# Token order in a linear-attention kernel: eight-token rows for k and r, values of two batches in chunk order, 64-row transposes

## The chip, the cores and the metric

The kernel runs on one core of one Trainium2 chip. The metric is device time in microseconds of one execution, the median of the runs. Five engines work side by side, each with its own instruction queue: PE (matrix products and transposes, into PSUM), DVE and ACT (vector work, both may read PSUM), POOL (vector work in SBUF) and SP (issues the DMAs). Within a queue the order is fixed; between queues semaphores order the work.

## The reference

A recurrent attention with a decaying state, then a token-mixing layer. Shapes: r, k, v, w are 4 batches x 8 heads x 768 tokens x 48, float32; the output is 4 x 768 x 384.

```python
state = zeros(B, H, D, D)
for t in range(S):
    cur = einsum('bhd,bhe->bhde', u[None] * k[:, :, t], v[:, :, t])
    y[:, :, t] = einsum('bhd,bhde->bhe', r[:, :, t], state + cur)
    state = w[:, :, t, :, None] * state + einsum('bhd,bhe->bhde', k[:, :, t], v[:, :, t])
x = y.transpose(0, 2, 1, 3).reshape(B, S, H * D)
wq = x @ w_q;  wk = x @ w_k
W_tok = (1 / sqrt(64)) * einsum('bsd,btd->bst', wq, wk)
out = maximum(einsum('bst,btd->bsd', W_tok, x), 0) @ w_out
```

## The kernel before

**Units.** A batch is cut into three units of 256 tokens; there are 12 units, n = 0 to 11. A unit holds two chunks of 128 tokens. In a chunk the recurrence is done as matrix products: with cumulative sums of log w, the weights exp(c) and exp(-c) are put on r and k, a masked 128 x 128 product per head gives the part inside the chunk, and a 48 x 48 state per head carries the rest. After the third unit of a batch the mixing layer of that batch is done.

**Loads** (L291 to L302). One DMA of 384 KB each brings w, k, r and v of a unit into the tiles wg, kg, rg, vg. A partition gets two neighbouring tokens of all eight heads, so a contiguous piece in memory is 2 x 48 x 4 = 384 bytes. For the batch in WHOLE (L233, batch 3) v comes at once, in chunk order, into vw: four DMAs, each into 64 partitions, in pieces of 192 bytes.

**Steps of a unit**, by the names of the step list, with the engine:

- ln (ACT, L453): log of w into lw. k16, r16 (L463) and v16 (L556): casts to bfloat16, on POOL mostly, of unit 0 on DVE.
- cw (PE): cumulative sums, 16 matmuls with 64 rows. ep, en (ACT, L491, L496): exp of them and of their negatives, to bfloat16. ep is written one token further on, since r needs the weight of the token before.
- kT, rT (PE, L502): k16 and r16 transposed, eight 128 x 128 transposes each. ks (ACT or DVE): copy of kT out of PSUM.
- qT (DVE, L522): r times k. RT (DVE, L531): r times ep. KT (POOL or DVE, L539): ks times en.
- vp (PE, L564): a product with the permutation PM that puts the two-token rows of v into chunk order, then VB (ACT): its copy out of PSUM. For batch 3 VB is cast from vw by POOL (L550) and there is no vp.
- dps (PE), dd: the part of a token's own key; Vd (POOL, L588): that part times VB.
- A (PE, L604), AM (DVE, L608): the products of a chunk, masked by US. kb (PE, L617), kd (L623): KT transposed back, scaled.
- sn (PE), SB (DVE, L654): the state. yi, ya (PE): both parts of the output of the recurrence. X (DVE, L712): their sum with Vd.
- xt (PE, L724), XT: X transposed. qk (PE), QK: products with w_q and w_k.
- For a batch: T, TS; then for each of its units mx (PE, L794), rl (relu, into MX), fp (PE, L812: times w_out), os (copy out), st (SP, L824: store of 384 KB).

In unit 11 and in part in unit 0 the steps are done by chunk, so that the pipeline starts and ends sooner; the suffix of a name such as AM.0.0 is the unit and the chunk. The matmuls with 64 or 48 rows use a part of the rows of PE's array, and two of them can be in the two halves.

**Order.** Each step is added to a plan with the engines it may run on. ALT (a string) picks the engine where there is a choice, RANK (a list with one number for each step) gives the place in its engine's queue. So the order of each queue is written out beforehand; a step whose input is late holds up what stands behind it. The durations in the plan (`dur`) are used to choose PSUM banks and the order in which the instructions are put into the program.

**Buffers.** PSUM is eight banks; a step takes one ("s") or two ("w"). The load tiles are rings of four, most others rings of two, so SP's loads wait for the last reader of the unit four before.

**Start.** Nine products with Z keep PE busy until the first data are there; twelve more of them (z) are spread over the order. POOL and DVE build the masks CM, US, PM and the identity.

Of the kernel before, what the change touches and what calls it, by code (L numbers as in the profile page):

```python
# [33 lines left out]
class Plan:  # L34
# [12 lines left out]
    def add(self, key, engs, fn, after=(), buf=None, reads=(), lag=None, mode=0, behind=None):  # L47
        e = next(iter(engs)) if len(engs) == 1 else next(self.alt, "")
        e = e if e in engs else next(iter(engs))
        if lag is None:  # L50
            lag = 260 if e == "E" else 80
        s = dict(key=key, engs=engs, eng=e, dur=engs[e], fn=fn, lag=lag, mode=mode, rank=0,
# [113 lines left out]
    0, 0, 0, 0, 0, 20, 0, 0, 21, 1, 3, 1, 0, 0, 2, 0, 0, 3, 0, 0, 6, 0, 0, 1, 1, 2, 3, 3, 2, 4, 6,  # L166
    6, 9, 3, 6, 4, 2, 5, 7, 5, 20, 10, 24, 12, 8, 10, 15, 8, 19, 11, 16, 9, 17, 11, 25, 12, 28,
    14, 30, 32, 35, 31, 18, 57, 30, 75, 38, 4, 0, 0, 5, 0, 0, 8, 0, 0, 7, 0, 0, 5, 4, 7, 14, 7, 8,
    18, 27, 9, 15, 16, 10, 6, 23, 14, 34, 17, 12, 38, 20, 41, 22, 26, 13, 33, 17, 36, 19, 42, 45,
    43, 46, 24, 64, 33, 77, 39, 9, 0, 0, 10, 0, 0, 13, 0, 0, 15, 0, 0, 13, 9, 20, 29, 15, 16, 37,  # L170
    44, 19, 25, 23, 13, 14, 47, 24, 51, 27, 20, 49, 26, 54, 29, 48, 25, 52, 27, 58, 68, 61, 65,
    35, 74, 37, 78, 40, 81, 43, 86, 44, 91, 47, 47, 0, 0, 88, 45, 97, 50, 51, 0, 0, 111, 56, 120,
    60, 54, 0, 0, 12, 0, 0, 11, 0, 0, 17, 0, 0, 16, 0, 0, 18, 11, 16, 40, 23, 22, 39, 56, 21, 31,
    30, 15, 17, 55, 29, 63, 34, 22, 60, 32, 67, 36, 53, 28, 66, 34, 71, 38, 70, 72, 73, 80, 41,
    89, 46, 101, 55, 14, 0, 0, 18, 0, 0, 21, 0, 0, 24, 0, 0, 21, 18, 35, 50, 28, 26, 59, 76, 31,
    40, 39, 33, 24, 84, 43, 82, 42, 28, 98, 53, 83, 44, 69, 36, 90, 47, 95, 52, 103, 104, 106,
    105, 57, 119, 63, 136, 68, 22, 0, 0, 19, 0, 0, 23, 0, 0, 27, 0, 0, 37, 19, 23, 79, 42, 41, 62,
    85, 32, 45, 46, 26, 27, 94, 49, 96, 51, 30, 102, 56, 93, 50, 92, 49, 100, 54, 108, 113, 115,
    112, 61, 129, 66, 139, 71, 145, 75, 153, 77, 160, 81, 50, 0, 0, 162, 82, 189, 97, 53, 0, 0,
    173, 88, 190, 98, 52, 0, 0, 26, 0, 0, 25, 0, 0, 30, 0, 0, 32, 0, 0, 48, 25, 31, 99, 53, 52,  # L180
    87, 110, 48, 60, 59, 32, 33, 116, 58, 122, 63, 40, 117, 62, 121, 64, 114, 57, 124, 65, 128,
    68, 132, 135, 133, 134, 72, 141, 74, 172, 87, 28, 0, 0, 29, 0, 0, 36, 0, 0, 33, 0, 0, 51, 29,
    37, 107, 54, 55, 109, 126, 58, 67, 69, 36, 35, 123, 62, 138, 69, 42, 137, 73, 144, 76, 125,
    66, 131, 71, 147, 77, 149, 150, 152, 151, 79, 164, 85, 180, 91, 35, 0, 0, 31, 0, 0, 37, 0, 0,
    34, 0, 0, 61, 34, 38, 127, 65, 64, 118, 130, 59, 70, 75, 41, 39, 143, 73, 140, 70, 47, 157,
    82, 146, 78, 142, 72, 155, 81, 166, 168, 169, 170, 88, 177, 92, 192, 101, 203, 103, 212, 105,
    218, 113, 55, 0, 0, 214, 106, 227, 111, 56, 0, 0, 222, 109, 230, 113, 57, 0, 0, 39, 0, 0, 41,
    0, 0, 38, 0, 0, 45, 0, 0, 46, 0, 0, 67, 43, 44, 148, 78, 76, 154, 158, 80, 84, 85, 48, 51,
    167, 84, 52, 176, 91, 165, 87, 163, 83, 175, 90, 179, 92, 182, 185, 184, 183, 95, 200, 102,
    211, 109, 42, 0, 0, 43, 0, 0, 40, 0, 0, 74, 46, 45, 156, 80, 79, 159, 161, 83, 86, 89, 49, 53,  # L190
    171, 86, 55, 191, 100, 181, 94, 178, 93, 187, 96, 194, 101, 197, 202, 198, 199, 104, 210, 104,
    215, 110, 48, 0, 0, 44, 0, 0, 49, 0, 0, 90, 50, 54, 186, 93, 94, 95, 96, 174, 188, 89, 99, 97,
    56, 98, 58, 57, 193, 100, 59, 60, 196, 102, 206, 105, 195, 99, 201, 103, 205, 208, 204, 207,
    209, 213, 106, 216, 108, 219, 221, 108, 112, 107, 217, 107, 220, 223, 111, 110, 224, 226, 225,
    114, 228, 115, 117, 231, 233, 114, 118, 58, 0, 0, 61, 0, 0, 229, 112, 116, 234, 235, 116, 117,
    59, 0, 0, 60, 0, 0, 232, 115, 118, 236, 237, 119, 119, 120, 62, 0, 0, 1, 2, 4, 5, 7, 8, 10,
    11, 12, 13, 21, 22,
]
ALT = "DDDPDAAAAAAPPDDAADAAPAAPAAADADAAAAAAPPDPAADADPAADADADAPPAPADDAAAAAAAAAPPDPAAADAPPDPAADAAPPAPAAAAAAADAAAAPPDPAAADPPDPADADPPAPPAADADADADDDAAADAAADDA"
# [5 lines left out]
def kernel(  # L205
# [27 lines left out]
    WHOLE = (3,)  # L233
# [18 lines left out]
    EW = 132  # L252
# [26 lines left out]
    ID16 = const([C, C], BF16, "ID16")  # L279
    IDU = const([C, C], BF16, "IDU")  # L280
# [4 lines left out]
    pos0 = const([C, 1], I32, "pos0")  # L285
    pos1 = const([C, 1], I32, "pos1")
# [8 lines left out]

    def load_whole(b, q, tl):
        n_ = H // 2 * NCH
        for j in range(2):
            nc.sync.dma_start(
                out=view(tl, q * n_ * D, [[D, n_], [1, D]], p0=64 * j, pn=64),  # L300
                in_=dataclasses.replace(v, offset=(b * H * S + j) * D + q * n_ * C * D,
                                        ap=[[D2, 64], [C * D, n_], [1, D]]))  # L302

    def setup():
# [9 lines left out]
        for j in range(2):  # L314
            nc.gpsimd.iota(pos0[ds(64 * j, 64), :], pattern=[[0, 1]], base=j,
                           channel_multiplier=2)
            nc.gpsimd.iota(pos1[ds(64 * j, 64), :], pattern=[[0, 1]], base=j + 1,
                           channel_multiplier=2)
# [3 lines left out]
        for c in range(2):  # L322
            for j in range(2):
                m = view(CM, j * C, [[64, 2], [1, 64]], p0=c * 64, pn=64)
                nc.gpsimd.affine_select(m, m, pattern=[[1, 2], [2, 64]], compare_op=ALU.is_ge,
                                        fill=0.0, base=-j, channel_multiplier=-2)
        nc.vector.memset(ID16, 0.0)
        nc.gpsimd.affine_select(ID16, ID16, pattern=[[1, C]], compare_op=ALU.not_equal, fill=1.0,
                                base=0, channel_multiplier=-1)
        for x in (tiles["lw"][0], tiles["k16"][0], tiles["r16"][0]):  # L330
            nc.vector.memset(view(x, D, pads), 0.0)
        for x in tiles["ep"]:
            nc.vector.memset(view(x, 0, [[EW, 8], [1, 1]]), 1.0)
        nc.vector.memset(US, 1.0)
        for j in range(2):
            m = view(US, 0, [[64, 2], [1, 64]], p0=j * 64, pn=64)
            nc.gpsimd.affine_select(m, m, pattern=[[1, 2], [2, 64]], compare_op=ALU.is_gt,
                                    fill=0.0, base=-j, channel_multiplier=-2)
# [4 lines left out]
        nc.vector.tensor_scalar_mul(US, US, gv)  # L343
# [5 lines left out]
    def permute():  # L349
        for c in range(2):  # L350
            for j in range(2):
                m = PM[ds(c * 64, 64), ds(j * C + j * 64, 64)]
                nc.gpsimd.affine_select(m, m, pattern=[[1, 64]], compare_op=ALU.not_equal,
                                        fill=1.0, base=0, channel_multiplier=-1)
# [14 lines left out]
    def bank():  # L369
        return Buf("s")  # L370
# [511 lines left out]
```

## Time and profile before

| | us |
|---|---|
| median of 3 runs | 106.43 (106.07 to 106.51) |
| span of the profiled execution | 104.4 |
| PE busy | 93.2 (89%) |
| PE weight loads | 69.4 (66%) |
| DVE busy | 84.4 (81%) |
| ACT busy | 80.6 (77%) |
| POOL busy | 69.3 (66%) |

The span is from the first to the last instruction of one profiled execution; the runs are timed from outside and are some 2 us longer. Busy time is the time in which an engine has an instruction running, whatever it waits for inside; matmuls overlap, so PE's figure says little of how near its peak it is. The page also cuts the span into 40 slices of 2.6 us. One row there is the TensorE clock that was granted, in tenths: it is 9 in all slices but one, at about 27 us, where it is 5. The DMA row is at 9 until the 24th slice with few exceptions and falls to 0 at about 81 us. The DMA queue that SP feeds moved 24.19 MB in 56,224 packets, 84.3% of the span of 16 DMA engines.

### The profile page before, as it was taken

The numbers are of one execution on the slowest core, as the hardware profiler recorded it, in microseconds if no ns is written. First come the engines' busy times: TensorE is split into PE (matmuls) and PEld (weight loads), VectorE is DVE, ScalarE is ACT, GpSimd is POOL, SyncE is SP. The second block draws the span as 40 slices with busy tenths as digits, with TensorE's granted clock in tenths as the row PEclk, the third lists the DMA queues.
The fourth block names the chain that finished last, engine by engine and source line by source line (L and its number), as shares of the span: only waits on it lengthen the run. The fifth ranks groups of instructions, "written<-read, shape, count | busy, mean of one in ns | idle before, by whom it ended". The sixth has DMA issues, their size and how long they took to land.

```text
span 104.4 us, 3964 instructions
## 1 busy us (share of the span) xinstructions
PE 93.2 (89%) x1651; PEld 69.4 (66%) x1652; DVE 84.4 (81%) x140; ACT 80.6 (77%) x122; POOL 69.3 (66%) x80
## 2 busy tenths in 40 slices
PE   5999899766998999999999899999999998999910
PEld 2356488544777786767886776887888596866500
DVE  6669996995789979979999889999899699695320
ACT  6348988759879869999999886899897954855830
POOL 6607666979998828959995699999975973000000
PEclk9999999999589999999999999999999999999999
DMA  1999999999999988999999799999993056004791
GB/s 26 296 324 325 325 318 234 309 290 237 301 342 295 246 228 206 303 254 243 310 294 256 195 264 276 244 179 172 292 349 137 0 220 238 0 9 181 295 359 72
DMA packets 56803, 24.65 MB, mean 236 GB/s; under 512 B 54480, under 2 KB 55632, under 8 KB 56784
## 3 DMA queue, kind: packets, MB, share of 16 engines
q1 hardware_dynamic: 56224, 24.19, 84.3%
q8 instruction: 13, 0.21, 0.8%
q10 hardware_dynamic: 560, 0.20, 0.7%
q14 instruction: 6, 0.05, 0.1%
HBM read 19.66 MB, written 4.72 MB: 234 GB/s over the span
## 4 chain that ended last, share of the span: by engine, by line
PE 74%; DMA 6%; POOL 5%; DVE 5%; issue 3%; ACT 2%; SPq 1%; POOLq 0%; DVEq 0%
PE PS L240 74%; DMA vg<-in_v_dram 6%; DVE KT L539 2%; POOL KT L539 2%; POOL v L556 2%; POOL Vd L588 1%; ACT ep L491 1%; ACT MX L396 1%; DVE RT L531 1%; DVE AM L608 1%; SPq L292 1%; DVE qT L522 1%; ACT os L384 0%; DVE Z L306 0%; POOL r L463 0%
## 5 line engine op out<-in xcount | busy, mean ns | idle before, releaser
L608 DVE TENSOR_TENSOR AM<-PS,US 128x1024 bf16<-128x1024 f32 x24 | 29.3, 1219 | 3.4 <-PE PS L240 3.2
L539 POOL TENSOR_TENSOR KT<-ks,en 128x1024 bf16<-128x1024 bf16 (+1 forms) x11 | 20.5, 1864 | 3.6 <-DVE ks L390 3.4
L588 POOL TENSOR_TENSOR Vd<-VB,dd 128x768 bf16<-128x768 bf16 (+1 forms) x14 | 18.1, 1294 | 1.3 <-ACT dd L384 1.2
L712 DVE SCALAR_TENSOR_TENSOR X<-PS,gx,Vd 128x768 bf16<-128x768 f32 (+1 forms) x13 | 12.4, 952 | 2.8 <-POOL Vd L588 1.4
L240 PEld LDWEIGHTS <-KT 48*128 48x128 bf16 (+1 forms) x272 | 10.9, 97 | 5.2 <-issue 2.4
L496 ACT ACTIVATE en<-PS 128x1024 bf16<-128x1024 f32 (+1 forms) x14 | 12.6, 898 | 2.0 <-PE PS L240 2.0
L491 ACT ACTIVATE ep<-PS 128x1024 bf16<-128x1024 f32 (+1 forms) x14 | 12.7, 919 | 1.3 <-ACT XT L384 0.6
L453 ACT ACTIVATE lw<-wg 128x768 bf16<-128x768 f32 x12 | 10.2, 848 | 4.5 <-DMA wg<-in_w_dram 4.4
L240 PE MATMUL PS<-wo,MX 128*128 128x384 bf16 x72 | 13.3, 326 | 0.0
L463 POOL CAST k<-kg 128x768 bf16<-128x768 f32 x11 | 9.0, 825 | 3.3 <-DMA kg<-in_k_dram 3.3
L384 ACT COPY os<-PS 128x768 f32<-128x768 f32 (+1 forms) x13 | 8.6, 680 | 2.5 <-PE PS L240 2.2
L463 POOL CAST r<-rg 128x768 bf16<-128x768 f32 x9 | 7.5, 835 | 4.3 <-DMA rg<-in_r_dram 2.3
L556 POOL CAST v<-vg 128x768 bf16<-128x768 f32 x9 | 7.4, 825 | 3.6 <-DMA vg<-in_v_dram 3.6
L240 PE MATMUL PS<-RT,KT 48*128 48x128 bf16 x192 | 9.7, 221 | 0.0
L240 PEld LDWEIGHTS <-MX 128*128 128x128 bf16 x72 | 6.5, 98 | 4.1 <-issue 0.3
L531 DVE TENSOR_TENSOR RT<-PS,ep 128x1024 bf16<-128x1024 bf16 (+1 forms) x14 | 8.4, 607 | 0.8 <-PE PS L240 0.5
L396 ACT ACTIVATE MX<-PS 128x768 bf16<-128x768 f32 (+1 forms) x11 | 8.2, 755 | 0.7 <-PE PS L240 0.6
L522 DVE TENSOR_TENSOR qT<-PS,ks 128x1024 bf16<-128x1024 bf16 x12 | 8.2, 681 | 0.4 <-issue 0.4
L240 PE MATMUL PS<-Z 128*128 128x512 bf16 x20 | 7.4, 511 | 1.2 <-DVE uT L309 1.2
L384 ACT COPY XT<-PS 128x768 bf16<-128x768 bf16 (+1 forms) x9 | 6.9, 765 | 2.0 <-PE PS L240 2.0
L240 PE MATMUL PS<-ID,r 128*128 128x128 bf16 x96 | 7.7, 226 | 0.4 <-POOL r L463 0.3
L240 PE MATMUL PS<-VB,AM 128*128 128x48 bf16 x192 | 7.9, 184 | 0.1
(83 smaller groups left out, 201.1 us busy)
## 6 DMA issues: line engine op xcount, KB each, us to landing
wg<-in_w_dram SPq DMA_DIRECT2D x12, 384.0 KB, 5.4
kg<-in_k_dram SPq DMA_DIRECT2D x12, 384.0 KB, 5.9
rg<-in_r_dram SPq DMA_DIRECT2D x12, 384.0 KB, 5.9
vg<-in_v_dram SPq DMA_DIRECT2D x9, 384.0 KB, 5.8
out_dram<-os SPq DMA_DIRECT2D x9, 384.0 KB, 3.0
vw<-in_v_dram SPq DMA_DIRECT2D x4, 288.0 KB, 6.2
out_dram<-os SPq DMA_DIRECT2D x5, 192.0 KB, 2.7
wof<-in_moe_w_out_dram SPq DMA_DIRECT2D x1, 576.0 KB, 5.4
```

What stands on the lines that cost most here:

```text
L240: return nc.tensor.matmul(o, l, rr, start=start, stop=stop, skip_group_check=True, is_transpose=trans)
L384: nc.scalar.copy(o, i)
L453: nc.scalar.activation(view(lw.tile, 0, [[64, H], [512, 2], [1, D]]), view(g["wg"].tile, 0, [[D2, H], [D, 2], [1, D]]), ACT.Ln, bias=0.0, ...
L463: op(view(o.tile, 0, [[64, H], [512, 2], [1, D]]), view(g[src].tile, 0, [[D2, H], [D, 2], [1, D]]))
L491: nc.scalar.activation(view(ep.tile, cs[0] * NP * EW + 66, [[EW, NP * len(cs)], [-65, 2], [1, 64]]), at(cw)[:, ds(cs[0] * 512, w_)], ACT.E ...
L496: nc.scalar.activation(en.tile[:, ds(cs[0] * 512, w_)], at(cw)[:, ds(cs[0] * 512, w_)], ACT.Exp, bias=0.0, scale=-1.0)
L531: nc.vector.tensor_tensor(view(RT.tile, cs[0] * 512, [[C, n4], [64, 2], [1, 64]]), view(at(rT, BF16), cs[0] * 512, [[C, n4], [64, 2], [1, ...
L539: x.tensor_tensor(KT.tile[:, cols], ks.tile[:, cols], en.tile[:, cols], ALU.mult)
L556: v16s = add(("v16", n), {"P": 826}, lambda e: nc.gpsimd.tensor_copy(view(v16.tile, 0, [[D, H], [DM, 2], [1, D]]), view(g["vg"].tile, 0, [ ...
L588: nc.gpsimd.tensor_tensor(Vd.tile[:, cols], VB.tile[:, cols], view(dd.tile, cs[0] * H, [[1, len(cs) * H], [0, D]]), ALU.mult)
L608: AMs[c] = add(("AM", n, c), {"D": 1221}, lambda e, c=c, A=A: nc.vector.tensor_tensor(view(AM[c].tile, 0, [[C, 8], [1, C]]), view(at(A), 0 ...
L712: nc.vector.scalar_tensor_tensor(view(X.tile, (2 * i + c0) * DM, [[DM, nc_], [1, DM]]), view(at(y), 0, [[512, nc_], [1, DM]]), gx, view(Vd ...
```

## The change

- k and r are loaded with eight neighbouring tokens of one head to a row (`load_runs`), two heads to a partition: contiguous pieces of 1536 bytes. w, and v where it isn't loaded whole, stay as they were.
- Within a chunk the tokens are therefore in another order: column 16 j + p is token 8 p + j. The masks CM, US and PM, the token numbers behind gx and gv and the moving operand of mx are made to match; the stores write rows of 1536 bytes in place of 3072.
- kT and rT become 16 transposes each, of 64 rows by 128, with a 64-column permuting identity IDP, into one pair of banks, kr, for both.
- ep is written in one piece, 16 columns further on; a new copy sh on POOL brings its last row of 15 columns to the front of each block. RT waits for sh.
- KT of units 0 and 11 is taken by DVE from PSUM directly, without ks (DIRECT).
- kb and xt get a second form ("e"): transposes in halves of 64 rows (48 for kb) into two banks. ALT chooses; kb takes it 9 times of 13, xt 6 of 13.
- WHOLE is batches 2 and 3: v of both is loaded in chunk order, by eight DMAs a batch, each into 16 partitions.
- The casts k16 and r16 of unit 0 go from DVE to POOL. RANK and ALT are new: one more k16 and two more r16 on POOL, KT 9 times on POOL instead of 11. In SP's queue the stores st.2.0, st.0.0 and st.3.0 stand ahead of the load of rg for unit 11, where it was st.0.0 alone.
- The setup has two iotas instead of four, some small integer steps on DVE for the token numbers, and IDP's masks instead of US's.

```diff
-    WHOLE = (3,)
+    DIRECT = (0, N - 1)
+    WHOLE = (2, 3)
...
-    EW = 132
+    EW = 144
...
+    def load_runs(b, i, tl, ap):
+        nc.sync.dma_start(
+            out=view(tl, 0, [[8 * D, 2], [1, 8 * D]]),
+            in_=dataclasses.replace(ap, offset=(b * H * S + i * U) * D,
+                                    ap=[[8 * D, U // 8], [2 * S * D, NP], [S * D, 2],
+                                        [1, 8 * D]]))
+
     def load_whole(b, q, tl):
...
+        nc.sync.dma_start(
+            out=view(tl, 0, [[D, H * NCH], [1, D]], p0=16 * q, pn=16),
+            in_=dataclasses.replace(v, offset=(b * H * S + q) * D,
+                                    ap=[[8 * D, 16], [C * D, H * NCH], [1, D]]))
...
+        nc.vector.tensor_scalar(US, tok, pos0, gv, ALU.is_gt, ALU.mult)
...
-                op(view(o.tile, 0, [[64, H], [512, 2], [1, D]]),
-                   view(g[src].tile, 0, [[D2, H], [D, 2], [1, D]]))
+                op(view(o.tile, 0, [[128, 8], [64, 2], [1, D]]),
+                   view(g[src].tile, 0, [[D, 8], [8 * D, 2], [1, D]]))
...
+            def f_sh(e, cs=cs, n4=n4):
+                nc.gpsimd.tensor_copy(view(ep.tile, cs[0] * NP * EW + 1, [[EW, n4], [1, 15]]),
+                                      view(ep.tile, cs[0] * NP * EW + C, [[EW, n4], [1, 15]]))
...
+        kr = wide()
+
+        def transposed(name, src, step, place):
             def f(e):
...
+                o = at(kr, BF16)
+                for j in range(8):
+                    for c in range(2):
+                        mm(view(o, c * 1024 + place + j * 16, [[C, NP], [1, 16]]),
+                           src.tile[ds(c * 64, 64), ds(j * 128, 128)],
+                           IDP[ds(c * 64, 64), :], trans=True)
...
+                if n in DIRECT:
+                    nc.vector.tensor_tensor(o, turned(0, cs[0], len(cs)), y, ALU.mult)
...
             x = add(("RT", n, cs[0]), {"D": 150 + int(n4 * C * 0.524)}, f_RT,
-                    [rTs] + [eps[c] for c in cs], RT, [rT, ep])
...
+                    [rTs] + [shs[c] for c in cs], RT, [kr, ep])
...
+                    for hh in range(2):
+                        mm(at(kb, BF16)[:, ds(hh * 1024 + cp * D, D)],
+                           KT.tile[ds(hh * 64, D), ds(cp * C, C)],
+                           ID16[ds(hh * 64, D), ds(hh * 64, D)], trans=True)
...
+                        for hf in range(2):
+                            rows = ds(hf * 64, 64)
+                            mm(at(xt, BF16)[:, ds(hf * 1024 + (dt * nc_ + k_) * 64, 64)],
+                               X.tile[rows, x], ID16[rows, rows], trans=True)
...
-                       view(QK.tile, ii * QS, [[64, 2], [C, 2], [1, 64]]),
+                       view(QK.tile, ii * QS, [[C, 2], [1, 16], [16, 8]]),
```

## The prediction

> **What bounds the kernel now.** I read the windows first, then the waits, then single instructions. Columns of the windows: stretch, its length, busy us (instructions) of PE, PEld, DVE, ACT, POOL, then granted clock, DMA share, GB/s.
>
> ```profile
> 10.68:30.00 19.32, 16.55 (x308) 12.38 (x308) 16.08 (x24) 15.69 (x23) 15.81 (x16) 0.91 1.08 292
> 30.00:60.00 30.00, 28.91 (x577) 22.74 (x574) 27.16 (x41) 27.24 (x36) 23.68 (x23) 1.00 0.99 260
> 60.00:80.00 20.00, 19.39 (x429) 16.16 (x424) 18.76 (x26) 17.21 (x28) 17.98 (x15) 1.00 1.00 248
> 80.00:90.11 10.11, 9.81 (x192) 7.62 (x190) 8.38 (x13) 6.91 (x13) 6.40 (x7) 1.00 0.32 122
> 90.11:104.40 14.29, 9.58 (x84) 6.13 (x81) 6.44 (x13) 7.38 (x15) 0.00 (x0) 1.00 0.45 167
> ```
>
> Three things are full at once: the DMA share is 0.99 to 1.08 until 80 us, PE is 96% busy from 30 us, DVE 91% from 30 to 60 and 94% to 80. No single engine owns the time. I therefore time the step that all meet, X.11.1 (DVE L712, start 90.11 us): every earlier DVE instruction stands ahead of it, and behind it lie 14.3 us of the last mixing. Between AM.0.0 (10.68) and X.11.1 DVE is busy 16.08 + 27.16 + 18.76 + 8.38 = 70.4 of 79.4 us and idle 9.0.
>
> ```profile
> DVE AM L608 <- PE PS L240: 3.2, 7, 1.1
> DVE X L712 <- POOL Vd L588: 1.4, 2, 0.9
> DVE X L712 <- PE PS L240: 1.3, 3, 0.7
> ```
> ```profile
> POOL v L556 <- DMA vg<-in_v_dram: 3.6, 4, 2.2
> POOL k L463 <- DMA kg<-in_k_dram: 3.3, 3, 1.8
> POOL r L463 <- DMA rg<-in_r_dram: 2.3, 2, 1.9
> ```
>
> DVE's idle time (first fence, waits of DVE: total us, times, longest) ends mostly on PE; POOL's (second) on loads. The longest wait for rg is the very last load: POOL sits until 79.52, where the cast of rg.11 starts. So a slow load delays POOL, POOL delays PE, PE delays DVE.
>
> **Loads.** Rates by packet size, as windows of the trace of before:
>
> ```profile
> 10.00:20.00 10.00, 8.95 (x179) 6.59 (x179) 8.77 (x14) 8.43 (x13) 7.27 (x9) 1.00 1.09 296
> 67.20:71.00 3.80, 3.63 (x74) 3.23 (x71) 3.64 (x6) 3.53 (x5) 3.80 (x4) 1.00 1.08 184
> 101.20:102.40 1.20, 0.00 (x0) 0.00 (x0) 0.00 (x0) 0.00 (x0) 0.00 (x0) 1.00 0.89 327
> ```
>
> The first moves 384-byte packets (two tokens), the second 192-byte packets of the chunk-order values, the third 1536-byte rows of the last stores. Divided by the DMA share: 272, 170 and 367 GB/s. A load of 393,216 bytes takes 1.45 us in two-token rows; in eight-token rows (8 x 48 x 4 = 1536 bytes) 1.07 us, if loads do as well as those stores: 24 loads x 0.38 = 9.1 us less. Bounds: nothing (272 GB/s again) to 9.1. Values of a batch in chunk order, 1.18 MB, take 6.9 us at 170 GB/s against 3 x 1.45 = 4.35 for three vg loads: 2.6 more for the batch that changes. In SP's queue two more stores now stand ahead of rg.11 (st.2.0 and st.3.0): 2 x 1.07 = 2.1 more. Net -9.1 + 2.6 + 2.1 = -4.4: rg.11 is cast from about 75.1 us instead of 79.5. SP issues 16 vw DMAs instead of 4, at about 0.5 us (the first kg issue at 1.28 took 0.57): 6 us more on SP, behind which wg.9 to wg.11 wait; hidden, since SP's loads at present take 1.1 to 1.2 us each because the queue is full.
>
> **PE.** Columns of the timeline: start, us, instruction; the step from one start to the next is what PE spends.
>
> ```profile
> 15.17 0.62 PE L240 MATMUL PS<-CM,lw 64*128 64x128 bf16 x16
> 15.63 0.26 PE L240 MATMUL PS<-SB,RT 48*128 48x48 bf16 x4
> 41.49 0.61 PE L240 MATMUL PS<-ID,k 128*128 128x128 bf16 x8
> 41.94 0.49 PE L240 MATMUL PS<-QK,TS 128*128 128x256 bf16 x3
> 82.91 0.40 PE L240 MATMUL PS<-RT,KT 48*128 48x128 bf16 x8
> 83.23 0.35 PE L240 MATMUL PS<-wk,XT 128*128 128x64 bf16 x6
> 84.55 0.40 PE L240 MATMUL PS<-RT,KT 48*128 48x128 bf16 x8
> 84.78 0.26 PE L240 MATMUL PS<-SB,RT 48*128 48x48 bf16 x8
> 84.98 0.57 PE L240 MATMUL PS<-VB,AM 128*128 128x48 bf16 x16
> ```
>
> Eight full transposes take 0.45 us (56 ns each). Sixteen 64-row matmuls of 128 columns take 0.46 (29 ns: two at a time). Eight RT,KT take 0.23 before another 48-row group and 0.32 before a full one: a change of row mode costs 0.09. So eight SB,RT of 48 columns take 0.20 - 0.09 = 0.11, 14 ns each. A 64-row transpose of 64 columns lies between 14 and 29; on the line through (48, 14) and (128, 29) it takes 17. kT and rT: 24 groups x (0.45 - 16 x 0.017) = -4.3 (bounds -5.4, and +0.2 at 29 ns). The order gives 9 of 13 kb steps the halved form (five with 4 columns blocks, four with 8): 52 blocks' worth of 56 ns become pairs of 14 to 17 ns, -1.3; 6 of 13 xt steps (six transposes, 0.33 to about 0.19): -0.8. The permuting matmuls vp of three units go (0.43 at 40.28, with a mode change): -1.1. Mode changes rise from 92 to 96: +0.4. Together about -7 us of PE's 93. mx (L795) reads its moving operand with a stride of 16 elements; no row shows one. From no cost (0.33 a step at 41.94) to double (the half rate that the first matmuls on Z show, 0.43 us apart against 0.22 later): 0 to +0.33 on each of 12, three of them in the tail. I take 0, since the clock alone explains the slow row.
>
> [...]
>
> **POOL.** It gains k16.0, r16.0 and one more r16 (+2.5 at 0.83 each), loses two KT net (20.5 us to 9 x 2.13 = 19.2: -1.3), v16 becomes VB at the same 0.83, and the new copy sh comes 14 times: 120 elements a row lie between the casts of 8 (0.19) and 192 elements (0.34), so 0.28, 0.23 for the four halves: +3.7. Sum +4.9 on 69.3. Each sh is queued behind casts that wait for loads, and RT (DVE), then A (PE), wait for it: this cover is what loads 4.4 us earlier pay for.
>
> **DVE and ACT.** Start: k16.0 and r16.0 leave DVE; kg.0 lands 0.4 us earlier, but DVE then does KT.0.0, ks.0, KT.0.1, kd.0.0, RT.0.0, qT.0 (four of 0.42, two of 0.68, each start some 0.05 before the last end) from the end of en.0.0 at 7.17: 2.8 to 2.9 us, AM.0.0 at about 10.1 instead of 10.68: **-0.6**. From there to X.11.1: ks.3, ks.6 and ks.9 go and ks.5 comes (-1.36), KT -0.25, RT.0.1 +0.42, one XT more +0.55, dd +0.33, TS and QK -1.1: **-1.4**. ACT takes two ks (+2.0), QK and TS (+2.4), and gives three VB, kd, two dd, r16 and XT (-6): lighter by 1.6.
>
> **Idle time of DVE** (9.0 us): PE has 7 us less to do, the loads come 4.4 us earlier, POOL is 4.9 fuller. Bounds: 0 and 5.9 (all three waits shown above). I take **-1.6**, nearer to nothing, as DVE would then be 90% busy, what it reaches now only in the middle. **Tail** of 14.3: two halved xt and earlier mx.8, **-0.4** (bounds -0.8 and +1.0, three strided mx).
>
> Sum: -0.6 - 1.4 - 1.6 - 0.4 = -4.0. The profiled execution has a span of 104.4, the median of the runs is 106.43, 2.0 more around it. Forecast: span 100.4, time **102.4**. Its own range, all bounds together: -8.7 to -1.0, 97.7 to 105.4.
>
> **Rivals.**
> *Sixteen-partition loads are slow (slower).* Each vw DMA now writes 16 partitions instead of 64. In the second window above, 64 partitions and half the packet cost 38% of the rate (170 against 272). Its forty slices, in GB/s:
>
> ```profile
> GB/s 251 235 226 174 150 119 105 95 95 125 117 117 152 202 379 226 226 212 226 232 224 218 186 138 113 115 133 137 178 156 158 210 212 228 232 212 220 208 230 192
> ```
>
> At the lowest, 95, a batch takes 12.4 us, 5.5 more than reckoned; for two batches the last load comes 2 x 5.5 - 4.4 = 6.6 us later than now, 86.1. The last vw.9 stands two transfers ahead, about 84.0, and from VB.9 on POOL still has 3 VB, k16, r16, two Vd, two sh and the halves of Vd.11: 5 x 0.83 + 2 x 1.48 + 0.46 + 1.62 = 9.2, to 93.2 instead of 87.1. X.11.1 follows at 93.3, 3.2 later than now, less 0.4 in the tail: 109.2. At 120 GB/s a batch takes 9.8 us, POOL ends at 88 and nothing is lost at this place. So it decides once the last load lands after about 83. For it: POOL can do nothing else first, as its queue is in order. Against it: half the slices show 200 to 232 GB/s on half the partitions. Time 109.2.
>
> [...]
>
> *POOL takes the gain (about even).* From k16.0 at 5.75 it has the 65.9 us that it does after 8.42 now, and 4.9 more: 76.6 without a wait. With the 12.8 us that it idles there now it ends at 89.4, 2.3 later than at present, and X.11.1 follows at 89.5: -0.6, less 0.4 in the tail, 105.4; any further 0.5 of waiting for sh's sources makes it no change. For it: in-order casts with sh behind them. Against: 9.2 of its idle time ended on loads.
>
> *The halved transposes do not pair (small gain).* PE saves 2 to 3 us, DVE's idle time stays: -0.6 - 1.4 = -2.0, the tail as now, 104.4. For it: no row has 64-row transposes. Against: CM,lw and SB,RT both pair.
>
> **Chances.** Forecast 0.52, no pairing 0.10, POOL 0.14, slow loads 0.24. Within 0.5% (0.53 us, what a measurement here can tell) lies half of POOL's. Faster: 0.52 + 0.10 + 0.07 = 0.69; same 0.07; slower 0.24. The range for 8 in 10 leaves out the far end of the slow loads and the forecast's best: 99.4 to 108.0.
>
> **What would show it.** Right: kg and rg about 1.1 us apart on the queue, the last cast of rg near 75 us; kT groups of 16 in about 0.27 us; sh near 0.28; AM.0.0 near 10; X.11.1 near 86.5. Wrong: vw at some 100 GB/s, VB waiting for vw for 5 us or more; RT waiting for sh; the granted clock at half for longer than the 3 us around 27 us in which PE, idle 1.59 us before, fell to it now.

## The result and the profile after

The changed kernel takes **121.75 us** (120.09 to 124.02, 4 runs) against 106.47 (106.07 to 106.99) of the kernel before on the same chip: ratio 1.143, 95% interval [1.132, 1.154]. Forecast were 102.4, with a range of 99.4 to 108.0: the direction was wrong, and the time lies outside the range. Ratios here and below leave disturbed runs out, which medians keep.

The span of the profiled execution is 120.1 us (before 104.4). The marker of the prediction, X.11.1, starts at 99.22 instead of 90.11. So 9.1 us were lost ahead of it and 6.6 behind it. Four lines of the page of the changed kernel: the granted clock and the GB/s of its forty slices, and two of the costliest groups (count, busy us, mean ns of one, idle time before and its releaser).

```profile
PEclk9998599999999955999999999997559999678699
GB/s 61 339 333 337 347 345 329 316 347 349 314 213 299 221 197 78 123 107 280 299 352 370 199 184 173 176 198 267 0 5 64 67 5 170 98 0 134 125 207 191
L250 PE MATMUL PS<-QK,TS 128*128 128x256 bf16 x36 | 18.3, 634 | 0.1
L419 ACT ACTIVATE MX<-PS 128x768 bf16<-128x768 f32 (+1 forms) x11 | 7.8, 723 | 12.6 <-PE PS L250 12.6
```

The third line was not among the costliest groups before. It is mx. Its 36 matmuls, three to each of the twelve steps, are now reported with 634 ns each, and ACT, which takes their results, waits 12.6 us for them. PE's timeline of the changed kernel around the first two steps (start, us, instruction):

```profile
40.27 0.37 PE L250 MATMUL PS<-VB,AM 128*128 128x48 bf16 x8
40.48 1.54 PE L250 MATMUL PS<-QK,TS 128*128 128x256 bf16 x3
41.84 0.50 PE L250 MATMUL PS<-VB,AM 128*128 128x48 bf16 x8
42.17 1.03 PE L250 MATMUL PS<-ID,KT 128*128 128x128 bf16 x8
43.13 0.61 PE L250 MATMUL PS<-RT,KT 48*128 48x128 bf16 x8
43.67 0.38 PE L250 MATMUL PS<-UB,qT 128*128 128x2 bf16 x8
43.91 1.54 PE L250 MATMUL PS<-QK,TS 128*128 128x256 bf16 x3
```

From the start of mx to the next instruction it is 1.36 us (40.48 to 41.84), where it was 0.33. From one of its matmuls to the next the trace has 440 and 460 ns; before it was 109. Twelve steps x 1.03 = 12.4 us. The waits of the changed kernel (us in total, times, longest) show who pays:

```profile
ACT MX L419 <- PE PS L250: 12.6, 10, 2.8
DVE SB L714 <- PE PS L250: 6.8, 6, 2.8
...
POOL k L489 <- DMA kg<-in_k_dram: 2.2, 2, 1.7
...
POOL VB L598 <- DMA out_dram<-os: 2.1, 1, 2.1
```

DVE's largest wait was AM's, 3.2 us; now SB waits 6.8 us: sn, which it follows, stands in PE's queue behind mx and the fp that comes after it (mx at 43.91, fp at 45.27, sn at 47.32, SB at 47.89 after 2.76 us of waiting). POOL's waits for loads have shrunk as forecast (kg 3.3 to 2.2, vg 3.6 to 0.3, none for rg), but a new one is there: VB waits 2.1 us. The releaser named is a store that was long done by then; the last packets of vw start at 80.63 us, and this cast (VB.9) at 81.40, so it is vw. The windows (stretch, length, busy us of PE, PEld, DVE, ACT, POOL, then granted clock, DMA share, GB/s) show the stages where the time went:

```profile
40.00:50.00 10.00, 10.00 (x120) 5.73 (x116) 5.41 (x9) 5.63 (x8) 6.12 (x6) 0.66 0.98 152
70.00:80.00 10.00, 9.48 (x215) 5.73 (x215) 8.53 (x12) 7.86 (x11) 9.14 (x9) 1.00 1.16 175
80.00:90.00 10.00, 9.88 (x171) 7.57 (x171) 6.11 (x8) 5.74 (x11) 5.67 (x8) 0.66 0.34 111
99.22:120.00 20.78, 16.98 (x84) 7.54 (x80) 6.06 (x12) 7.37 (x15) 0.00 (x0) 0.84 0.37 134
```

The same stretch in the kernel before:

```profile
40.00:50.00 10.00, 9.91 (x194) 7.38 (x196) 9.17 (x17) 9.48 (x12) 8.81 (x8) 1.00 1.01 259
```

At 40 to 50 us PE has no idle time at all, and yet only 120 instructions run on it where 194 did, and DVE is busy for 5.41 us where it had 9.17. At 80 to 90 us it is much the same. Five mx steps lie behind X.11.1 (100.27, 101.73, 106.8, 108.16 and 111.97): 5 x 1.03 = 5.2 of the 6.6 us lost there. The DMA share is 1.16 at 175 GB/s while vw is loaded (70 to 80 us).

Two causes are to be told apart, and a remainder: the operand of mx, the loads of vw, and what the rest of the change does without these two.

### The profile page after: what moved, and what is told of

Same layout as the page of the kernel before. It is cut to its first block, busy times and chain, and to the rows that moved or that the text cites. A ratio compares the mean times of both kernels' runs of the same rounds, so it can differ in the third digit from the quotient of the medians.

```text
span 120.1 us, 4515 instructions
## 1 busy us (share of the span) xinstructions
PE 105.5 (88%) x1916; PEld 68.6 (57%) x1916; DVE 82.8 (69%) x144; ACT 80.3 (67%) x119; POOL 74.1 (62%) x93
## 4 chain that ended last, share of the span: by engine, by line
PE 73%; DVE 11%; DMA 4%; issue 4%; ACT 3%; POOL 1%; SPq 0%; DVEq 0%; POOLq 0%
PE PS L250 73%; DMA kg<-in_k_dram 4%; DVE qT L559 3%; DVE AM L656 2%; ACT ks L407 2%; DVE RT L573 1%; DVE KT L583 1%; DVE ks L413 1%; DVE X L772 1%; ACT os L407 1%; DVE KT L580 1%; POOL k L489 1%; ACT lw L479 1%; SPq L306 0%; DVE SB L714 0%
## 5 line engine op out<-in xcount | busy, mean ns | idle before, releaser
L583 POOL TENSOR_TENSOR KT<-ks,en 128x1024 bf16<-128x1024 bf16 x9 | 19.2, 2128 | 4.4 <-ACT dd L407 1.6
L250 PE MATMUL PS<-QK,TS 128*128 128x256 bf16 x36 | 18.3, 634 | 0.1
L419 ACT ACTIVATE MX<-PS 128x768 bf16<-128x768 f32 (+1 forms) x11 | 7.8, 723 | 12.6 <-PE PS L250 12.6
L250 PE MATMUL PS<-wo,MX 128*128 128x384 bf16 x72 | 15.9, 374 | 0.0
L772 DVE SCALAR_TENSOR_TENSOR X<-PS,gx,Vd 128x768 bf16<-128x768 f32 (+1 forms) x13 | 12.4, 954 | 3.7 <-PE PS L250 2.1
L528 ACT ACTIVATE en<-PS 128x1024 bf16<-128x1024 f32 (+1 forms) x14 | 12.4, 902 | 1.4 <-PE PS L250 0.7
L519 ACT ACTIVATE ep<-PS 128x1024 bf16<-128x1024 f32 (+1 forms) x14 | 12.6, 906 | 0.6 <-PE PS L250 0.4
L479 ACT ACTIVATE lw<-wg 128x768 bf16<-128x768 f32 x12 | 10.1, 843 | 3.3 <-DMA wg<-in_w_dram 3.3
L250 PEld LDWEIGHTS <-MX 128*128 128x128 bf16 x72 | 7.5, 110 | 7.6 <-issue 4.6
L714 DVE TENSOR_TENSOR SB<-PS,ep 128x192 bf16<-128x192 f32 x20 | 7.0, 352 | 6.8 <-PE PS L250 6.8
L489 POOL CAST k<-kg 128x768 bf16<-128x768 f32 x12 | 10.4, 863 | 2.2 <-DMA kg<-in_k_dram 2.2
L250 PE MATMUL PS<-RT,KT 48*128 48x128 bf16 x192 | 10.7, 234 | 0.0
L250 PE MATMUL PS<-Z 128*128 128x512 bf16 x21 | 8.3, 479 | 1.2 <-DVE low L336 1.2
L489 POOL CAST r<-rg 128x768 bf16<-128x768 f32 x11 | 9.1, 825 | 0.0
L250 PE MATMUL PS<-SB,RT 48*128 48x48 bf16 x160 | 6.9, 183 | 2.3 <-DVE AM L656 1.0
```

The source lines that it names most:

```text
L250: return nc.tensor.matmul(o, l, rr, start=start, stop=stop, skip_group_check=True, is_transpose=trans)
L479: nc.scalar.activation(view(lw.tile, 0, [[64, H], [512, 2], [1, D]]), view(g["wg"].tile, 0, [[D2, H], [D, 2], [1, D]]), ACT.Ln, bias=0.0, ...
L489: op(view(o.tile, 0, [[128, 8], [64, 2], [1, D]]), view(g[src].tile, 0, [[D, 8], [8 * D, 2], [1, D]]))
L519: nc.scalar.activation(view(ep.tile, cs[0] * NP * EW + 16, [[EW, n4], [1, C]]), at(cw)[:, ds(cs[0] * 512, w_)], ACT.Exp, bias=0.0, scale=1.0)
L528: nc.scalar.activation(en.tile[:, ds(cs[0] * 512, w_)], at(cw)[:, ds(cs[0] * 512, w_)], ACT.Exp, bias=0.0, scale=-1.0)
L583: x.tensor_tensor(o, view(ks.tile, cs[0] * 512, dims), y, ALU.mult)
```

## The experiments

Times are medians, each with the ratio to the kernel before on the same chip and its 95% interval. Three chips were in use: one for e1 to e3, b2 and b3, one for b1, e6 to e8 and e12 to e14, one for e15 to e17. Between them only the ratios compare.

| run | edit | us | ratio |
|---|---|---|---|
| b1_stride_alone | before, mx's operand alone | 119.08 | 1.117 [1.110, 1.125] |
| e1_mx_contiguous | after, mx contiguous | 110.35 | 1.050 [1.041, 1.060] |
| e2_vw_128_partitions | after, vw by 128 partitions | 122.97 | 1.158 [1.145, 1.172] |
| e3_both | both | 105.71 | 0.996 [0.990, 1.002] |
| e7_contiguous_spread_vw | e1, vw by 8 partitions 16 apart | 114.81 | 1.074 [1.065, 1.084] |
| e6_both_and_early_z | e3, ten more z early | 105.67 | 0.999 [0.995, 1.004] |
| e8_both_and_start | e6, PM and r16.0 moved | 105.88 | 1.000 [0.995, 1.004] |
| e12_both_less_pool | e3, three KT from POOL to DVE | 108.42 | 1.033 [1.025, 1.040] |
| e13_start_less_pool | e12 with e8's start | 109.60 | 1.036 [1.025, 1.046] |
| e15_less_dve | e3, half of AM in three units left out (DVE) | 105.69 | 0.988 [0.978, 0.999] |
| e16_less_pe | e3, a third of some fp and qk left out (PE) | 105.90 | 0.990 [0.985, 0.995] |
| e17_less_pool | e3, some sh and half of some Vd left out (POOL) | 105.26 | 0.989 [0.985, 0.994] |

b2 (113.6), b3 (113.24) and e14 (125.09) have no interval.

### The operand of mx: e1, b1, b2, b3

In e1 mx reads its columns one after the other again; rl, which copies the result out of PSUM in any case, puts the tokens in order.

```diff
-                       view(QK.tile, ii * QS, [[C, 2], [1, 16], [16, 8]]),
+                       QK.tile[:, ds(ii * QS, U)],
...
-                    view(at(mx), cs[0] * C, [[U, NK], [1, w_]])), [mxs], MX, [mx])
+                    view(at(mx), cs[0] * C, [[U // len(cs), NK * len(cs)], [1, 16], [16, 8]])),
+                    [mxs], MX, [mx])
```

> The changed kernel with one edit: mx reads its moving operand contiguously, and the token order is put right by the relu copy rl, which reads PSUM with a step of 16. Theory S (the strided moving operand is the cost: 36 matmuls at 0.45 us instead of 0.11, and the lower granted clock that follows them): each mx step back to 0.33 us, PE 12 us lighter, granted clock 0.97 or more, time 105 to 110 us. Theory V (the loads into 16 partitions are the cost): mx gets faster but VB still waits for vw, time 115 us or more. If rl pays for the strided read instead, its mean rises from 0.8 us towards 2.

The same step of PE's timeline in e1:

```profile
42.99 0.49 PE L250 MATMUL PS<-QK,TS 128*128 128x256 bf16 x3
```

The step is 109 ns a matmul again, X.11.1 starts at 93.94 and the time falls from 121.75 to 110.35, by 11.4 us (by the ratios, 0.093 x 106 = 9.8). The permuting read by rl costs nothing that shows: on ACT its 768 columns take 811 ns in e1 and took 812 in the kernel before, on DVE its halves 552 and 555. b1 does the opposite, the stride and nothing else in the kernel before (its columns, and those of b2 and b3, come in another order):

```diff
-                       view(QK.tile, ii * QS, [[64, 2], [C, 2], [1, 64]]),
+                       view(QK.tile, ii * QS, [[C, 2], [1, 16], [16, 8]]),
```

> The kernel before, with nothing changed but mx's moving operand, which is read with the changed kernel's steps ([[C, 2], [1, 16], [16, 8]] in place of [[64, 2], [C, 2], [1, 64]]); the columns of mx, and so the tokens of the output, come in another order. Theory (the stride costs by itself, whatever the rest): 12 steps x 1.03 us = 12.4 on PE, nearly all of it on the path as in the changed kernel, 117 to 120; 440 to 460 ns from one 256-column matmul to the next. Rival (the stride only costs together with the fuller PE or the emptier loads of the changed kernel): under 112.

119.08 us: this one line, in an otherwise untouched kernel, costs 13.3 us against the median of 105.81 of the kernel before on that chip, and 0.117 x 106 = 12.4 by the ratio, which is what 12 x 1.03 on PE gives. Which steps cost what, b2 and b3 were to show.

> The kernel before with only the read of mx changed: units 0 and 1 step 1 (contiguous over 128), 2 and 3 step 2, 4 and 5 step 4, 6 and 7 step 8, 8 and 9 step 16, 10 and 11 step 32 elements of two bytes; the output tokens are in another order. Theory S: 0.33 us a step at steps 1, rising to 1.36 at 16; at 2 to 8 between these, and 1.36 at 32. Time 108 to 114. If the slow mx of the changed kernel comes from something else (its banks, its neighbours), all twelve take 0.33 us and the time stays at 106.

In b2, other than expected, each whole batch took one step (2, 4, 16 and 32 elements); these gave 115, 207 to 229, 440 to 460 and 412 to 431 ns. b3 has all six:

```diff
-                       view(QK.tile, ii * QS, [[64, 2], [C, 2], [1, 64]]),
+                       view(QK.tile, ii * QS, [[C, 2], [1, step], [step, C // step]]),
```

> The kernel before with mx's moving operand read at six steps, one for each two units: 1, 2, 4, 8, 16 and 32 elements of 2 bytes (the columns come in another order). The run that was to do this gave whole batches one step by a slip and left 1 and 8 out. Theory (each element is fetched by itself from 8 elements on, and the price is then full): 109, 115, 215, 430 to 460, 440 to 460, 410 to 435 ns from one 256-column matmul to the next. Rival (8 elements, 16 bytes, share a fetch, and the price is full only at 16): 8 elements at 210 to 230.

PE's timeline of b3, one line for each step, 1, 2, 4, 8, 16 and 32 elements in this order:

```profile
42.50 0.49 PE L240 MATMUL PS<-QK,TS 128*128 128x256 bf16 x3
...
52.42 0.50 PE L240 MATMUL PS<-QK,TS 128*128 128x256 bf16 x3
...
72.42 0.84 PE L240 MATMUL PS<-QK,TS 128*128 128x256 bf16 x3
...
90.57 1.52 PE L240 MATMUL PS<-QK,TS 128*128 128x256 bf16 x3
...
95.64 1.54 PE L240 MATMUL PS<-QK,TS 128*128 128x256 bf16 x3
...
103.01 1.45 PE L240 MATMUL PS<-QK,TS 128*128 128x256 bf16 x3
```

From one start to the next: 109, 115, 208 to 229, 431 to 453, 439 to 460 and 415 to 431 ns for 256 columns. Of the steps tried, 2 elements cost 6 ns more than 1, 4 elements twice the time, and 8, 16 and 32 elements (16, 32 and 64 bytes) about four times. The theory's numbers hold and the rival's (8 elements at 210 to 230) do not; how the elements are read, alone or several together, no run shows. The price did not follow the granted clock: in the changed kernel the step at 43.91, where the granted clock is 0.50 (41.8 to 48.5 us), takes 440 and 460 ns like that at 70.15 at full clock. A contiguous step at half clock (e1, 80.19, in slices of 5 and 7 tenths) takes 189 to 213 in place of 109.

### The loads of vw: e2, e3, e7, e14

In e2 a DMA brings one head for all 128 partitions, in place of one token of each eight for 16 partitions. Pieces are still 192 bytes, eight DMAs a batch; the values come in token order, which is not the order of the rest, so e2 and all that build on it (e3, e6, e8, e12, e13, e15 to e17) work on other numbers. The pieces of one DMA also lie otherwise in memory: consecutive tokens, where the changed kernel takes every eighth.

```diff
-            out=view(tl, 0, [[D, H * NCH], [1, D]], p0=16 * q, pn=16),
-            in_=dataclasses.replace(v, offset=(b * H * S + q) * D,
-                                    ap=[[8 * D, 16], [C * D, H * NCH], [1, D]]))
+            out=view(tl, q * NCH * D, [[D, NCH], [1, D]]),
+            in_=dataclasses.replace(v, offset=(b * H + q) * S * D,
+                                    ap=[[D, C], [C * D, NCH], [1, D]]))
```

> The changed kernel with one edit: each of the eight vw loads of a batch fills all 128 partitions for one head, same bytes, same 192-byte packets, same number of loads; the values land in the order of tokens instead of the permuted one. Theory S: the loads of a batch take 6 to 7 us instead of 11, but the time falls by 0 to 4 us only, to 118 to 122. Theory V: time below 110 us.

> Both edits: mx contiguous with the order put right in rl, and vw loads into 128 partitions (values in the order of tokens). Theory S plus V: 101 to 105 us, below the kernel before. If the new order, sh or the halved transposes cost time of their own: 106 us or more, with DVE or PE waiting for POOL.

In the packet records of the traces a 192-byte packet takes 27.4 ns in the mean in the changed kernel, 15.5 in e2 and 15.3 in e3; over 16 engines that is 21.1, 11.9 and 11.8 us for the two batches. Issue to landing of a vw DMA (us: least, median, most), first in the changed kernel, then in e3:

```profile
DMA to landing us min/median/max: 5.2/6.9/10.4
```
```profile
DMA to landing us min/median/max: 2.7/4.2/6.7
```

By itself this is worth nothing: e2 is not faster than the changed kernel (1.158 against 1.143). With mx mended it is worth 4.6 us (110.35 to 105.71; by the ratios, 0.054 x 106 = 5.8). The place is VB.9 on POOL: in e1 it waits 2.9 us and starts at 79.92, in e3 it starts at 76.41 without a wait, 3.5 earlier, and X.11.1 follows 3.6 earlier (90.38 against 93.94). The slow mx had hidden the slow loads.

e7 tries to have both the order and the speed: two DMAs for each one, with 8 partitions that lie 16 apart. Each reads consecutive tokens.

```diff
+        def spread(x):
+            return dataclasses.replace(x, ap=[[16 * x.ap[0][0], 8]] + [list(d) for d in x.ap[1:]])
+        for x in (2 * q, 2 * q + 1):
+            nc.sync.dma_start(
+                out=spread(view(tl, 0, [[D, H * NCH], [1, D]], p0=x, pn=1)),
+                in_=dataclasses.replace(v, offset=(b * H * S + 8 * x) * D,
+                                        ap=[[D, 8], [C * D, H * NCH], [1, D]]))
```

> e1 (contiguous mx, rl puts the tokens in order) with vw loaded by 16 DMAs a batch of 8 partitions each, 16 apart, in place of 8 DMAs of 16 neighbouring partitions; 192-byte pieces as before, and the values are in the right order. Theory (neighbouring partitions are what slows the vw loads): 7 us a batch or less and X.11.1 near 90.5, 105.7 as e3. Rival (few partitions, or the strided pieces in memory, slow them): 110 or more, as e1.

The packets took 16.0 ns, but the time was worse, 114.81 (1.074 against e1's 1.050). The windows of e1 and then e7, with vw of batch 2 in them, show that the loads themselves were not faster:

```profile
40.00:50.00 10.00, 8.99 (x233) 6.61 (x227) 8.62 (x14) 8.54 (x13) 9.93 (x10) 1.00 1.06 165
```
```profile
40.00:50.00 10.00, 8.99 (x233) 6.61 (x227) 8.62 (x14) 8.53 (x13) 9.93 (x10) 1.00 0.69 153
```

From 44 to 54 us, where nearly all packets are of vw, e1 moves 124 GB/s at a DMA share of 1.17 and e7 99 at 0.52. So e7's short packets come with DMA engines that are idle half the time, and they settle nothing: neighbouring partitions, their small number and the order of the pieces in memory all remain as what slows the loads of the changed kernel. The view of the tile vw in e7 (SP's time for one DMA in ns: least, median, most) says why the time was worse:

```profile
L321 SPq DMA_DIRECT2D vw<-in_v_dram x32: 588/621/1826, 36.7 to 78.4; - x32
...
  DMA out_dram<-os: 5.1, 1
```

An issue takes SP 0.62 us, 16 of them 9.9 us, longer than their transfer of 12.3 / 2 = 6.2 us, and VB waits 5.1 us (again put down to a store). Neither the theory nor the rival had this in numbers. e14 puts these pairs between other loads in SP's queue, those of batch 2 from rg.5 on and those of batch 3 from wg.8 on, with e12's and e8's edits besides:

```diff
+FIRST = {('vw', 6, 0): 22.5, ('vw', 6, 1): 23.5,
...
+         ('vw', 9, 6): 46.5, ('vw', 9, 7): 47.5}
```

> e13 with the values in the right order: vw by 8 partitions 16 apart as in e7, whose packets took 15 ns but whose 16 DMAs a batch followed each other at SP's issue time of 0.62 us; here each pair of them stands between two other loads in SP's queue. Theory (with the issue time behind other loads' transfers nothing waits for vw): VB.6 and VB.9 without a wait over 1 us, within 1 us of e13. Rival (SP's queue becomes the bound: 32 + 42 issues x 0.6 = 44 us in the first 65): rg.11 is cast after 85 us, 108 or more.

125.09 us. The longest wait of e14 between 30 and 100 us:

```profile
POOL k L494 <- DMA kg<-in_k_dram: 11.2, 3, 6.0
```

SP now needed 1.2 to 4.5 us for a pair. Between 27 and 65 us its 35 issues took 35.6 of the 38 us: its queue became the bound as the rival had it, and kg came late. From 32 to 34 us, with other loads in the queue (DMA share 1.24), the packets of these spread loads took 33.5 ns in the mean, so spreading the partitions does not keep them short. The order of the values and fast loads were not brought together here; no version with the output of the kernel before was found that beats it.

### The missing 4 us: e6, e8, e12, e13, e15, e16, e17

With both mended, e3 is level with the kernel before (0.996), where the sum said 4 us less. In e3 AM.0.0 starts at 12.20 (forecast 10.1), PE is idle from 6.0 to 7.6, and the granted clock is at half from 8 to 15 us. So the start was tried first.

e6 adds ten z behind cw.0, kT.0 and rT.0; e8 also has PM's masks first on POOL, and r16.0 first on DVE (a letter of ALT, not shown, moves it there).

```diff
-    130, 124, 30, 128, 15, 234, 7, 35,
+    130, 124, 30, 128, 15, 234, 7, 35, 2, 2, 2, 2, 2, 2, 3, 3, 4, 4,
...
-WARM = 12
+WARM = 22
+FIRST = {('pm',): 0, ('r16', 0): 0}
```

> e3 (contiguous mx, vw by 128 partitions, values in token order) with ten more products with Z: six right after cw.0, two after kT.0, two after rT.0. Theory (part of the missing 4 us is the granted clock, at half from 8 to 16 us because PE is idle from 5.9 to 7.6 us): PE full before 8 us, the granted clock 9 from the third slice to the tenth, X.11.1 near 89, 104.3. Rival (the start is bound by k16, r16, PM and sh on POOL, the clock costs nothing): AM.0.0 within 0.3 us of 12.2 and 105.7, as e3.

> e6 with PM's masks ahead of k16.0 in POOL's queue, where POOL is idle, and r16.0 on DVE in place of POOL. Theory (the start is late because POOL's casts and masks stand in a row ahead of rT and sh): AM.0.0 from 12.2 to about 10.8, X.11.1 1 us earlier than e6's, about 103.5. Rival (a late start is caught up later, loads decide): X.11.1 within 0.4 us of e6's.

AM.0.0 is at 11.55 in e6 and at 11.18 in e8. That alone says little: the nine profiles with the start of e3 have it anywhere from 10.74 (e2) to 12.43 (e17), as the first kg lands earlier or later. Counted from the start of k16.0 it is 4.68 us in e6 and 4.74 in e8, and 4.75 (the changed kernel) to 5.65 (e17) in the nine, with a median of 5.26, so the edits shorten the start by some 0.5 us. In e6 the granted clock also stayed full until past 18 us. But the times did not move: 0.999 and 1.000, and X.11.1 starts at 90.52 in e6. What the start gains is lost again later; both theories fall. POOL, without a gap from 66 to 81 us in e3, was next: e12 moves three KT from it to DVE (three letters of ALT, not shown; FIRST sets their places).

```diff
+FIRST = {('KT', 8, 0): 72.5, ('KT', 9, 0): 82.5, ('KT', 10, 0): 85.5}
...
-            s_["rank"] = x
+            s_["rank"] = FIRST.get(s_["key"], x)
```

> e3 (contiguous mx, vw by 128 partitions, values in token order) with KT of units 8, 9 and 10 on DVE in place of POOL: 3 x 2.13 = 6.4 us less on POOL, which e3's trace shows without a gap from 66 to 81 us, and 3 x 0.69 = 2.1 us more on DVE. Theory (POOL took the gain, the rival of the prediction): PE gets its operands earlier, X.11.1 from 90.4 to 88 or less, 103.5 or less. Rival (PE itself is full from 50 us on and sets the end): X.11.1 within 0.5 us of 90.4, 105.7.

> e12 with e8's start (ten more products with Z, PM's masks ahead of k16.0, r16.0 on DVE). Theory (the start's 1 us was lost at POOL alone): 0.7 to 1 us under e12, 102.8 or less. Rival (PE is full in the middle): as e12.

Both theories fall here too: e12 is slower than e3 by 3.7% of the time before (1.033 against 0.996), and e13 no faster than e12. The three KT on DVE in e12, then POOL in the same stretch:

```profile
63.61 1.60 DVE L585 TENSOR_TENSOR KT<-ks,en 128x1024 bf16<-128x1024 bf16 x1
...
72.92 0.68 DVE L585 TENSOR_TENSOR KT<-ks,en 128x1024 bf16<-128x1024 bf16 x1
...
76.34 1.07 DVE L585 TENSOR_TENSOR KT<-ks,en 128x1024 bf16<-128x1024 bf16 x1
```
```profile
63.19 1.48 POOL L638 TENSOR_TENSOR Vd<-VB,dd 128x768 bf16<-128x768 bf16 x1 [1.42 <-ACT dd L409]
64.61 1.28 POOL L600 CAST VB<-vw 128x768 bf16<-128x768 f32 x1
...
75.77 0.28 POOL L526 COPY ep<-ep 128x120 bf16<-128x120 bf16 x1 [5.30 <-ACT dd L409]
76.05 2.06 POOL L600 CAST VB<-vw 128x768 bf16<-128x768 f32 x2
```

Only the middle one, during which POOL sits idle, takes the 0.68 us reckoned; the others take 1.60 and 1.07, so DVE got 3.35 us more and not 2.1, and POOL's cast beside the first took 1.28 in place of 0.82. So e12 does not say what taking work from POOL alone does. The last three runs leave out work on one engine and add none: half of AM's columns in three units (e15), a third of fp and qk in some units (e16), sh of five units and half of Vd in three (e17).

```diff
-                view(AM[c].tile, 0, [[C, 8], [1, C]]), view(at(A), 0, [[C, 8], [1, C]]),
+                view(AM[c].tile, 0, [[C, 4 if n in (7, 8, 9) else 8], [1, C]]),
...
+                            if m < 6 and kt == 1:
+                                continue
...
+                if n in (6, 7, 8, 9, 10):
+                    return
...
-                cols = ds(cs[0] * DM, len(cs) * DM)
+                part = 2 if n in (7, 8, 9) else 1
+                cols = ds(cs[0] * DM, len(cs) * DM // part)
```

> e3 (contiguous mx, vw by 128 partitions, values in token order) with work left out on DVE: AM of units 7, 8 and 9 is done for half of its columns, 6 x 0.6 = 3.6 us less. Theory (with the two slow things mended DVE sets the pace, as e12, 2.1 us more on DVE, was 2.7 us slower than e3): X.11.1 from 90.4 to 87.5 or less, 102.5 to 103.5. Rival (PE or POOL sets it): within 0.6 us of e3's 105.7.

> e3 with work left out on PE: one of the three parts of each sum in fp of the first six units mixed and in qk of units 7 to 9 is not added, 6 x 0.33 + 3 x 0.16 = 2.5 us less. Theory (DVE sets the pace): within 0.6 us of e3's 105.7. Rival (PE sets it, 95% busy from 50 us on): 103.5 or less.

> e3 with work left out on POOL, and none added elsewhere: sh of units 6 to 10, and half the columns of Vd of units 7 to 9, 5 x 0.28 + 3 x 0.72 = 3.6 us less. Theory (DVE sets the pace): within 0.6 us of e3's 105.7. Rival (POOL takes the gain, as the prediction's rival had it): 103.5 or less.

AM went from 29.1 to 25.9 us, PE's busy time from 89.5 to 87.0, Vd and sh together from 22.1 to 18.4. All three runs give about the same, and little: ratios of 0.988, 0.990 and 0.989 against e3's 0.996, that is 0.6 to 0.8 us for 2.5 to 3.7 us of work, a fifth to a quarter of it. No theory holds: none of DVE, PE and POOL sets the end alone. What does is not shown. That the three are nearly level fits; but the loads (DMA share 0.93 to 1.11 in e3 until 70 us) and ACT were not lightened, and no run lightened two engines at once. The intervals of these three overlap that of e3, so the size of the gain is uncertain; that none of them comes near 3 us is not.

## Why the prediction was wrong, point by point

**The step that failed: the strided operand of mx.** The prediction had the point in its list: "no row shows one. From no cost (0.33 a step at 41.94) to double ... 0 to +0.33 on each of 12 ... I take 0, since the clock alone explains the slow row." It measured +1.03 a step, three times the upper bound. Of the 15.3 us lost, e1 gives back 11.4 (9.8 by the ratios), and b1, the stride alone, costs 12.4 by its ratio. The working was at fault in two places. The row taken as the far end (matmuls on Z, 0.43 us apart) had nothing to do with strides, so it bounded nothing. And the value was taken at the end that the row, once put down to the clock, left over; that the clock explains it was the author's estimate, and no view shows it: the windows of before give a granted clock of 1.00 from 0 to 10 us, with those matmuls in it. "Three of them in the tail" was short as well: four lie behind X.11.1 in the kernel before (92.32 to 96.62), five in the changed one.

**The loads.** Rows of 1536 bytes did in the main what was reckoned: POOL's waits for loads went from 9.2 us to 3.6 in e3, and there rg.11 lands at 76.6, 2.9 us before the 79.5 of the kernel before, where 4.4 were reckoned. But POOL casts it only at 80.15, when its own queue comes to it, and not at 75.1. The values were under-sized: 6.9 us a batch were taken, 10.5 measured (21.1 / 2). The rival "sixteen-partition loads are slow" was right in that they are slow (27.4 ns a packet against 15.3 in e3) and in the place: VB.9 waits in POOL's queue (2.1 us in the changed kernel, 2.9 in e1). Its price, 109.2, lies near the 110.35 of e1, in which it stands nearly alone, in part by luck: it took 12.4 us a batch, and it counted on savings of which e3 shows little. In the changed kernel itself it was covered by mx. That it is the sixteen partitions that make them slow is not shown: no run here has the order in memory changed alone.

**PE without mx.** The halved transposes do pair at full clock: 16 in 0.24 us, 15 ns each (17 taken; the changed kernel at 72.14). Two starts lie 3 to 4 ns apart, and the next pair comes 29 ns after the first. So the rival that they don't pair falls. PE's busy time in e3 is 89.5 where 93.2 less 7 were expected. Half clock at 8 to 15 and 25 to 32 us may take part of it, but e6, with a mean clock of 0.98 and ten more z, also has 89.5.

**POOL.** 69.3 + 4.9 = 74.2 were forecast, 74.1 measured; sh took 0.28 to 0.29 and 0.23. Right to the tenth.

**DVE, idle time, tail.** Measured on e3, which has only these terms left: the start came out +1.5 (AM.0.0 12.20 against 10.68) in place of -0.6, the stretch to X.11.1 78.2 us against 79.4, -1.25 in place of -3.0, the tail 13.2 against 14.3, -1.1 in place of -0.4. The sum is -0.8 of span where -4.0 stood. The start was mis-sized: from k16.0 to AM.0.0 it allowed 10.1 - 5.75 = 4.35 us, and e3 takes 5.46. k16.0 and r16.0 are slower on POOL (0.83 against 0.56), and DVE waits for PE 0.70 us before ks.0 and 0.66 before AM.0.0; sh.0.0 is not in the way, as it ends at 10.24, before RT.0.0 (10.52) has its turn on DVE. The first kg also lands later in e3 (k16.0 at 6.74 and not 5.75), which differs from run to run. But e6 and e8 show that even a shorter start is not kept. What failed is adding up the savings of three engines of which none alone is the bound: e15 to e17 put what 3 us on one engine are worth at some 0.7. Why e3 keeps so little of the 4 us stays open beyond that. The rival "POOL takes the gain" named 105.4, and e3 has 105.7, yet e17 shows that POOL alone does not take it.

**The granted clock.** That it would be at half for long, in the list of what would prove the prediction wrong, came about: it is 0.66 at 40 to 50 and 80 to 90 us, and 0.90 in the mean against 0.98. In e1 the slices at 43 us are full again. But b1, with the same strided steps at 41.77 and 43.59, has a granted clock of 1.00 from 31 to 98 us, so the stride by itself did not bring the clock down there, and what did in the changed kernel is not shown. And b1 loses its 12 us in runs with a mean clock of 0.97 to 0.98, as the kernel before has it, so the loss does not need the slower clock.

## What to carry to other kernels

A bound taken from a row that shares nothing with the operation is not a bound: for an access pattern that no row shows, time one instruction of it alone, or allow the worst that was seen here (four times the price, 415 to 460 ns in place of 109, at steps of 8 to 32 elements), or put the permutation into a copy that is made anyway, as rl did at no cost (811 ns in e1, 812 before). A transfer of the same bytes in the same pieces may still take 1.8 times as long for the partitions it writes or the order it reads in (27.4 against 15.3 ns a packet), and splitting it finer may only move the cost to the queue that issues it (0.62 us an issue in e7). A mean packet time says little without the DMA share beside it: packets were short in e7 (16.0 ns) with the engines half idle (0.52). Where three engines are nearly full in the same stage, don't add up their savings; here a single one's was worth a fifth to a quarter of itself.

## What the runs showed of the hardware that was not expected

- PE's moving operand (b3): 256 bf16 columns in 109 ns at steps of 1 element, 115 at 2, 208 to 229 at 4, 431 to 453 at 8, 439 to 460 at 16, 415 to 431 at 32. At step 16 half clock made no difference (440 and 460 in the changed kernel, at a clock of 0.50 and of 1.00).
- The granted clock fell to half in a stretch in which PE had no idle time by the profile (10.00 of 10.00 us busy at 40 to 50 us, clock 0.66), with the strided matmuls in it; with contiguous ones at the same place (e1, 1.00) it did not, nor with strided ones in the kernel before (b1, 1.00). The cause is open.
- In e12 a KT on DVE with two operands in SBUF took 0.68 us while POOL was idle, and 1.60 and 1.07 while POOL worked; a cast on POOL beside the first took 1.28 us where others take 0.82. These are three KT and one cast; what makes them slower no run shows.
- 192-byte packets took 27.4 ns into 16 neighbouring partitions (the changed kernel), 17.2 into 64 (the kernel before) and 15.3 into 128 (e3), mostly with the DMA engines full (DMA share 1.16, 1.08 and 0.93 to 1.11). Into 8 that lie 16 apart they took 16.0 with the engines half idle (e7, 0.52), and 33.5 with a full queue (e14, 32 to 34 us).
